# Upsampled attention and token/channel mixer on one core: a table of importance and transfer costs for the list scheduler of the first batch

## The chip, the cores and the metric

The kernel runs on one core of a Trainium2 chip. The metric is device time in microseconds (us) of that core for one execution; lower is better. TensorE is called PE below (PEld where it loads weights), VectorE DVE, ScalarE ACT, GpSimd POOL, and SyncE SP. SP only issues transfers here, and ACT issues four more for each batch.

## The reference

Per batch (8 of them, sequence 576, 8 heads of 64): attention over queries, keys and values averaged in groups of four, repeated back to full length, plus attention in a band of seven positions, and then a mixer over tokens and channels.

```python
out_d = sm_attn(q_d, k_d, v_d)                 # means of 4: 144 x 144 per head
out_up = np.repeat(out_d, factor, axis=2)
mask = np.abs(pos[:, None] - pos[None, :]) < factor
...
x = out_up + out_local                         # (576, 512) per batch
h = np.maximum(xt @ w_tok1, 0.0) @ w_tok2      # token mixing, 576 -> 256 -> 576
u = x + h.transpose(0, 2, 1)
h2 = np.maximum(u @ w_ch1, 0.0) @ w_ch2        # channel mixing, 512 -> 1536 -> 512
return (u + h2).astype(np.float32)
```

## The kernel before

**Work of a batch.** `pooled` (pr 0 to 3) is the averaged attention of two heads each: scores `sd`, `exp` into `pd`, transposes `td`, copy `ptd`, products `ad`, and the result `od`, which four transfers from ACT's queue write into the tiles `vw` of the windowed values. `local` (t 0 to 4) is the band for a tile of 128 rows: scores `sc`, softmax in `P`, transposes `pT`, products `av` with `vw`, and a copy to `x`. `mix` has four generators: `splits` (`x` into high and low parts `xh`), `products` (token products `t1` with W1, then `t2` with W2), `takes` (`hid`, then `u` and its maxima `umx`) and `scaled` (the scaled f16 pair `uh`). The channel products are `c1` (C1 with `uh`, twelve groups f for each half ch of the columns) and `c2` (C2 with `h`). In the trace, `t1` and `t2` both read as `t`, `c1` and `c2` as `c`; buffer numbers are left out.

**Weights.** They arrive as 64-bit words and are turned to f32 once, in the first batch, by `to_f32`: ACT scales the upper words (L210), POOL does two passes (L213, L216), DVE joins them (L221). There are nine pieces of the token weights (W0 to W4 are W1, W5 to W8 are W2; then a cast on ACT, L239, and a difference on DVE, L241), twelve tiles of C1 (raw `C1`, result `CW`) and twelve of C2 (result `CX`, the last `CY`). A tile of C1 or C2 then has its norm summed on PE (`C_sum`), and once a scale is known, `parts` splits it into an f16 pair (L293 on ACT, L295 on DVE). POOL also adds up the averaged values `vr` to `vd` (L409, L410), and for every batch but the first the averaged queries and keys (`pool_q`, L435 to L443). All of this, for the first two batches, shares the five queues with the first batch's attention.

**Order.** Instructions run on each engine in the order in which the program issues them. For the first batch, 75 generators ("streams") are run by a list scheduler, `drive`. A stream yields `step(engine, us, *needs)`: the engine, a cost, what must have been made. `drive` keeps a planned clock for each engine, takes the steps that may go, finds the earliest start, and among those on the same engine within `PATIENCE` of it takes the first of the list; the streams stand in the order of `"LMCTWUDSAmPHaQh"`. Where PE has a planned gap ahead of a product, `keep_busy` fills part of it with products of junk (`busy`). `drive` ends when the first batch's channel mixing and the second's first `uh` are done; from there on, each batch's channel products are run with the next batch's attention in between, a fixed share after each product.

**Streams.** L0 averages the first batch's queries, L1 loads its values, L2, L4 and L5 load the token weights, C1 and C2, L3 its windowed values. C0 to C11, D0 to D11 and W0 to W8 turn tiles of C1, C2 and the token weights; S0 and T0 scale C1 and C2. A0 to A8 are the first batch's attention, M0 to M3 its mix, P0, P1 and Q0 its channel products, U0 to U2 what follows those. H0 loads the second batch, a0 to a8 and m0 to m3 are its attention and mix, h0 loads the third. SP's planned cost is 0.1 us a step, and a load of several transfers is one step.

Of the kernel before, what the change touches and what calls it, by code (L numbers as in the profile page):

```python
# [28 lines left out]
LIVE = 3  # L29
SG = 4  # L30
PATIENCE = 0.15


@with_exitstack
def tile_ups_attention_mixer(ctx, tc, qk, vw, vr, w1, w2, c1, c2, out):

    nc = tc.nc
    B, _, S = out.shape
# [85 lines left out]

    clock = dict(A=2.0, G=5.0, V=2.0, P=0.0, S=0.0, D=0.0)
    now = [0.0]
    free = {k: {i: 0.0 for i in range(n)} for k, n in SLOTS.items()}
    held = {}  # L130
# [21 lines left out]

    def drive(streams, until):

        items = [[g, next(g, None), 0.0] for g in streams]
        driven[0] = True
        while not all(u in made for u in until):
            some = []
            for it in items:
                if it[1] is None or not may(it[1]):  # L160
                    continue
                e, us, needs, at, take, give = it[1]
                if any(not free[k.split('>')[0]] for k in take):
                    continue
                t = max([clock[e], it[2] if at is None else at] + [made[n] for n in needs]
                        + [min(free[k.split('>')[0]].values()) for k in take])
                some.append((t, it))
            best = min(some, key=lambda x: x[0])
            best = next(x for x in some if x[0] <= best[0] + PATIENCE and (x[0] == best[0] or x[1][1][0] == best[1][1][0]))
            t, it = best  # L170
            e, us, _, _, take, give = it[1]
            if e == "P" and ("uh", 0, 1) not in made and free["g"]:
                keep_busy(min(8, int((t - clock["P"]) * 0.6 / 0.22)))
            if e == "P" and ("uh", 0, 0) not in made:
                us *= 1.2
            now[0] = max(now[0], t)
            for x in take:
                k = x.split(">")[0]
                i = now_in[k] = min(free[k], key=free[k].get)
                del free[k][i]  # L180
                held.setdefault((x, None if ">" in x else id(it)), []).append(i)
            clock[e] = t + us
            it[2] = t + us + 0.3
            for x in give:
                i = held[x, None if ">" in x else id(it)].pop(0)
                free[x.split(">")[0]][i] = it[2]
            try:
                it[1] = it[0].send(it[2])
            except StopIteration:
                it[1] = None  # L190
        driven[0] = False
        for k, n in SLOTS.items():
            first = min(free[k], key=free[k].get) if free[k] else [i for (x, _), v in held.items() for i in v if x.split(">")[0] == k][0]
            now_in[k] = (first - 1) % n
        return [it for it in items if it[1] is not None]
# [28 lines left out]
    def weight_loads(pieces, tag, name):  # L224
        raws = {}
        for i, (src, n) in enumerate(pieces):
            yield step("S", 0.1, *([(name, "read", i - BUFS[tag])] if i >= BUFS[tag] else []))
            raws[i] = T([src.shape[0], 2 * n], U32, tag, f"{name}{i}_raw")
            nc.sync.dma_start(raws[i], src)
            made[name, "raw", i] = fetched(src.shape[0] * n * 8)  # L230
            made[name, "raw"] = raws
# [87 lines left out]
    class Second(Channel):  # L319
# [22 lines left out]
        def loads(self):  # L342

            self.raws = made["C2", "raw"] = []
            for i in range(NF):
                if i < 4:
                    yield step("S", 0.1, *(("tile", 0, t) for t in range(len(TILES))))
                    t = T([128, S + KW], F32, "qk", f"C2_raw{i}")[:, :1024].bitcast(U32)
                else:
                    if i % 2 == 0:  # L350
                        yield step("S", 0.1, *(("av", 0, t) for t in range(len(TILES))), *([("C2", "read", i - 4), ("C2", "read", i - 3)] if i >= 8 else []))
                        two = T([128, 2, 1024], U32, "vw", f"C2_raws{i}")
                    t = two[:, i % 2]
                nc.sync.dma_start(t, u32(c2[i]))
                self.raws.append(t)
                made["C2", "raw", i] = fetched(2 ** 19)
# [28 lines left out]
    def load_v(st):  # L385
        st.vd = T([G, 2, H, D + 1], F32, "vd", f"vd{st.b}")
        nc.gpsimd.memset(st.vd[:, :, :, D:D + 1], 4.0)
        ts, arrives = {}, {}

        def fetch(i):  # L390
            pr, g = divmod(i, 2)

            tag = "w" if st.b > 1 else "x" if st.b or i < BUFS["x"] else "xh"
            ts[i] = T([G, 4, 128], F32, tag, f"vr{st.b}_{i}")
            nc.sync.dma_start(ts[i], vr[st.b, g, pr].rearrange("p (r c) -> p r c", r=4))
            arrives[i] = fetched(147e3)

        early = {0: 8, 1: 5}.get(st.b, 0)
        if early:
            yield step("S", 0.1, *([("mixed", 0)] if st.b else []))  # L400
        for i in range(early):
            fetch(i)
        for i in range(8):
            pr, g = divmod(i, 2)
            if i >= early:
                fetch(i)
            t = ts.pop(i)
            e = yield step("G", 1.25, at=arrives[i])
            nc.gpsimd.tensor_add(t[:, 0:2], t[:, 0:2], t[:, 2:4])  # L409
            nc.gpsimd.tensor_add(st.vd[:, g, 2 * pr:2 * pr + 2, :D], t[:, 0].rearrange("p (h d) -> p h d", d=D),  # L410
                                 t[:, 1].rearrange("p (h d) -> p h d", d=D))
            make(("v", st.b, i), e)
# [39 lines left out]
    def pooled(st, pr):  # L452
# [33 lines left out]
        for par in range(2):  # L486
            for g in range(2):
                for kg in range(2):
                    nc.tensor.matmul(ps[:, g, par], pt[:, par, kg, G * g:G * g + G], st.vd[:, kg, 2 * pr + par],  # L489
                                     start=kg == 0, stop=kg == 1)  # L490
        if pr == 0:
            st.od = T([G, 2, 2, 4, D], F32, "od", f"od{b}")
        r = T([G, 2, 2], F32, "sm", f"rd{b}_{pr}")
        e = yield step("V", 0.65, give=one)
# [1 line left out]
        nc.vector.reciprocal(r, r)  # L496
        nc.vector.tensor_tensor(st.od[:, :, :, pr], ps[:, :, :, :D], r.unsqueeze(3).to_broadcast([G, 2, 2, D]),
                                ALU.mult)
        if pr == 3:
            yield step("A", 0.2, ("vw", b), at=e)  # L500
            for h in range(2):
                for par in range(2):
                    nc.scalar.dma_start(st.vw[h][64 * par + 1 + WB:64 * par + KB],
                                      st.od[:, h, par].rearrange("p a d -> p (a d)"))
            make(("full", b), e, 3.0)
        make(("pair", b, pr), e)

    def local(st, t):
# [38 lines left out]
        yield step("A", 0.59, give=one)  # L547
        nc.scalar.copy(pt, ps[:, :4 * n].rearrange("p (hp s) -> p hp s", hp=4))
        make(("tile", b, t), e)
        e = yield step("P", 0.8, ("full", b), ("vw", b), take="gg")  # L550
        ps = P2(f"av{b}_{t}")
        for hp in range(4):
            for j in range(nb):
# [28 lines left out]
    def mix(st):  # L582
# [19 lines left out]
        def products():  # L602
# [8 lines left out]
            for ch in range(2):  # L611
                s0, N = CHUNKS[ch]
                for c in range(4):
                    e = yield step("P", 1.2, ("W", "y", NT + 3), ("hid", b),
                                   *([("over", b - 1, 0)] if b and ch == 0 else []), take="" if c % 2 else f"gg>{b}")
                    if c % 2 == 0:
                        banks[ch, c // 2] = P2(f"t2_{b}_{ch}_{c}")
                    ps = banks[ch, c // 2][:, c % 2, :N]
                    for i, t in enumerate(OF_CHUNK[ch]):
                        o, n = TILES[t][0] - s0, TILES[t][1]  # L620
                        nc.tensor.matmul(ps[:, o:o + n], xf(t)[:, 128 * c:128 * c + 128], ident[:n, :n],  # L621
                                         start=i == 0, stop=False, is_transpose=True, skip_group_check=True)
                    for k in range(2):
                        mm3(ps, lambda a: st.hid[k][:, a, 128 * c:128 * c + 128],
                            lambda a: W2[k][:, a, s0:s0 + N], False, k == 1, skip_group_check=True)
                    make(("t2", b, ch, c), e)
# [71 lines left out]

    def ahead(b):

        yield step("S", 0.1, *([("C2", "read", i) for i in range(4)] + [("pair", 0, 3)] if b == 1 else []))
        st = load(b)
        if b > 1:
            load_w(st)
        yield from pool_all(st)
        yield from load_v(st)
        if b == 1:
            yield step("S", 0.1, *(("C2", "read", i) for i in range(4, NF)))
            load_w(st)

    def side(b):
# [94 lines left out]
        return mixes[b]  # L806

    def windows(st):
        yield step("S", 0.1)
        load_w(st)  # L810

    last = len(TILES) - 1
    with tc.manual_schedule():
# [19 lines left out]
        group["P"] = products[:2]  # L833
        group["Q"] = products[2:]
        group["h"] = [lazily(lambda: ahead(2), ("x", 1, last))]
        streams = [x for k in "LMCTWUDSAmPHaQh" for x in group[k]]
        left = drive(streams, [("over", 0, 1)] + [("uh", 1, 0)] * (B > 1))

    def rest(items):
# [105 lines left out]
```

## Time and profile before

| what | us |
|---|---|
| median of three runs | 963.13 (960.53 to 964.6) |
| span of the profiled execution | 963.2 |
| PE busy in it | 920.6 (96%) |
| DVE, ACT, POOL busy | 440.5, 314.3, 228.5 |

No own time of the profiled execution is listed beside its span; the span agrees with the median within 0.1 us. In the page's second part, each digit is the busy share of a fortieth of the span, some 24 us. A row of the timeline gives start, duration, engine, line, operation, result<-operands, the count, and in brackets the engine's idle time just before and what ended it. A row of a table of windows gives the stretch, its length, then busy time and instructions of each engine, PE's granted clock, the share of the DMA engines and GB/s.

### The profile page before, as it was taken

What the parts mean: (1) busy time and instruction counts of PE and PEld (TensorE: products, weight loads), DVE (VectorE), ACT (ScalarE), POOL (GpSimd) and SP (SyncE); (2) the same over time, 40 slices, a digit from 0 to 9 for tenths busy, and PEclk for the clock granted to TensorE, in tenths of its full rate; (3) what the DMA queues carried; (4) which work ended last, traced back from release to release, by engine and by line L of the source; (5) the groups of instructions that cost most, each with busy time, mean ns of one, the idle gap of its engine ahead of it and who ended that gap; (6) DMA issues with size and microseconds to landing.
All of it is one profiled execution on the core that took longest, in us unless ns stands there. A gap on an engine that the chain in (4) does not pass through costs nothing. (4 is left out here: it accounts for less than half of the span.)

```text
span 963.2 us, 25951 instructions
## 1 busy us (share of the span) xinstructions
PE 920.6 (96%) x11426; PEld 710.8 (74%) x11426; DVE 440.5 (46%) x1058; ACT 314.3 (33%) x723; POOL 228.5 (24%) x361
## 2 busy tenths in 40 slices
PE   6887799999999999999999999999999999999998
PEld 3465577877877788677877778777876778777876
DVE  6777787325352354324453253524453254523221
ACT  2464545214242152314232152413423143422110
POOL 5599960420321003400223003400124000000000
PEclk9777999999999999999999999999999999999999
DMA  8773330620250002500232002500034000000000
GB/s 245 235 278 98 119 80 15 176 64 20 75 155 25 21 20 66 163 14 15 63 126 58 21 9 80 166 7 21 27 82 140 15 14 26 14 1 21 19 12 28
DMA packets 28224, 68.31 MB, mean 71 GB/s; under 512 B 3504, under 2 KB 14000, under 8 KB 26864
## 3 DMA queue, kind: packets, MB, share of 16 engines
q1 hardware_dynamic: 25552, 64.30, 22.0%
q10 hardware_dynamic: 2560, 2.36, 0.9%
q8 instruction: 89, 1.46, 0.6%
q14 instruction: 23, 0.19, 0.1%
HBM read 54.85 MB, written 9.44 MB: 67 GB/s over the span
## 5 line engine op out<-in xcount | busy, mean ns | idle before, releaser
L114 PE MATMUL c<-uh,CW 128*128 128x256 f16 (+1 forms) x2304 | 308.5, 286 | 1.6 <-DVE h L744 1.0
L114 PE MATMUL c<-h,CX 128*128 128x256 f16 (+1 forms) x2304 | 306.9, 286 | 0.0
L114 PEld LDWEIGHTS <-CW 128*128 128x128 f16 x2304 | 216.5, 98 | 68.5 <-issue 15.8
L114 PEld LDWEIGHTS <-CX 128*128 128x128 f16 x2304 | 216.5, 98 | 58.3 <-issue 1.4
L744 DVE SCALAR_TENSOR_TENSOR h<-c,h 128x320 f16<-128x320 f32 (+1 forms) x192 | 87.3, 455 | 161.7 <-ACT h L742 161.6
L742 ACT ACTIVATE h<-c 128x320 f16<-128x320 f32 (+1 forms) x192 | 78.4, 409 | 184.6 <-PE c L114 183.9
L409 POOL TENSOR_TENSOR vr<-vr 72x256 f32<-72x256 f32 x64 | 47.4, 741 | 340.2 <-ACT ptd L483 266.5
L770 DVE SCALAR_TENSOR_TENSOR u<-c,io,u 128x256 f32<-128x256 f32 (+1 forms) x64 | 33.0, 515 | 132.2 <-PE c L114 132.1
L646 ACT COPY u<-t 128x256 f32<-128x256 f32 (+1 forms) x64 | 25.4, 399 | 149.4 <-PE t L114 117.4
L435 POOL TENSOR_TENSOR qs<-qk 128x288 f32<-128x288 f32 x56 | 39.9, 712 | 135.2 <-DMA qk<-in_qk_dram 131.4
L114 PE MATMUL t<-xh,W 128*128 128x512 f32 (+1 forms) x240 | 69.6, 425 | 1.6 <-DVE xh L599 1.4
L648 DVE TENSOR_REDUCE umx<-t 128x1 f32<-128x256 f32 (+1 forms) x64 | 29.2, 457 | 84.8 <-ACT u L646 69.6
L114 PE MATMUL t<-W,hid 128*128 128x256 f32 (+1 forms) x384 | 68.0, 313 | 0.0
L114 PEld LDWEIGHTS t<-W,hid 128*128 128x128 f32 x384 | 54.0, 192 | 2.2
L114 PEld LDWEIGHTS t<-xh,W 128*128 128x128 f32 (+1 forms) x240 | 44.6, 196 | 14.0 <-issue 2.4
L562 ACT COPY x<-av 128x512 f32<-128x512 f32 (+1 forms) x40 | 23.1, 577 | 82.8 <-PE av L557 80.9
L473 ACT ACTIVATE pd<-sd,nmd 72x144 f32<-72x144 f32 x128 | 38.9, 376 | 28.5 <-DVE nmd L468 23.1
L489 PE MATMUL ad<-vd,ptd 72*72 72x65 f32 x512 | 39.4, 229 | 5.1 <-issue 4.7
L489 PEld LDWEIGHTS ad<-vd,ptd 72*72 72x72 f32 x512 | 37.4, 146 | 7.0 <-issue 5.4
L557 PE MATMUL av<-vw,pt 47*32 47x64 f32 x2304 | 35.6, 229 | 5.8 <-DMA vw<-od 3.8
L557 PEld LDWEIGHTS av<-vw,pt 47*32 47x32 f32 x2304 | 27.8, 108 | 16.2 <-issue 8.2
L599 DVE TENSOR_TENSOR xh<-x,xh 128x512 fp32r<-128x512 f32 (+1 forms) x40 | 31.2, 784 | 17.0 <-ACT xh L597 16.9
(107 smaller groups left out, 905.0 us busy)
## 6 DMA issues: line engine op xcount, KB each, us to landing
qk<-in_qk_dram SPq DMA_DIRECT2D x32, 579.0 KB
vw<-in_vw_dram SPq DMA_DIRECT2D x32, 351.0 KB
vr<-in_vr_dram SPq DMA_DIRECT2D x64, 144.0 KB
C_raw<-in_c_dram SPq DMA_DIRECT2D x16, 512.0 KB
out_dram<-u SPq DMA_DIRECT2D x32, 160.0 KB
C_raws<-in_c_dram SPq DMA_DIRECT2D x8, 512.0 KB
out_dram<-u SPq DMA_DIRECT2D x32, 128.0 KB
vw<-od ACTq DMA_DIRECT2D x32, 72.0 KB
```

What stands on the lines that cost most here:

```text
L114: nc.tensor.matmul(ps, lhs(a), rhs(c), start=first and i == 0, stop=last and i == 2, **kw)
L409: nc.gpsimd.tensor_add(t[:, 0:2], t[:, 0:2], t[:, 2:4])
L435: nc.gpsimd.tensor_add(two, x[:, :, 0:2], x[:, :, 2:4])
L473: nc.scalar.activation(pd[:, par, g], s[:, par, g], AF.Exp, bias=nm[:, par, g:g + 1], scale=0.125 / 16)
L489: nc.tensor.matmul(ps[:, g, par], pt[:, par, kg, G * g:G * g + G], st.vd[:, kg, 2 * pr + par], start=kg == 0, stop=kg == 1)
L557: nc.tensor.matmul(ps[QB * j:QB * j + QB, par, D * hp:D * hp + D], pt[p, hp, QB * j:QB * j + QB], st.vw[h][p, g, D * hp:D * hp + D], start ...
L599: nc.vector.tensor_tensor(xh[:, 1], xf(t), xh[:, 0].bitcast(F32), ALU.subtract)
L646: nc.scalar.copy(u, ps)
L648: nc.vector.tensor_reduce(umx[ch][:, c:c + 1], ps, axis=AX.X, op=ALU.max, apply_absolute_value=True)
L742: nc.scalar.activation(ht[:, 0], ps, AF.Relu)
L744: nc.vector.scalar_tensor_tensor(ht[:, 1], ps, 0.0, ht[:, 0], ALU.max, ALU.subtract)
L770: nc.vector.scalar_tensor_tensor(us[c], banks[c], io, us[c], ALU.mult, ALU.add)
```

## The change

It gives each stream a place in a table, `ORDER`. Among the ready steps on the best one's engine within `PATIENCE`, `drive` now takes the one that stands first in the table instead of first in the list, and the rule that a step on any engine goes first if it starts equally early is gone. SP's steps cost `ISSUE` = 0.65 us, and a load of several transfers is a step for each (`C2.loads`, and `load_v` of the first two batches). SP's planned clock starts at 3.0. ACT's step that issues the four transfers of `od` is planned with 2.9 us instead of 0.2 for the first two batches, with the arrival 2.0 us later. Three needs are written out, since the order may now differ: `od` of the other heads, all four pieces of W2, and the tile `od` made by whichever head comes first.

```diff
+ORDER = ("C7 C8 P1 D3 D7 T0 A1 D10 a7 U0 L2 M0 L5 W1 A2 A3 m1 U1 C9 a1 C4 D4 L0 D9 W6 W0 M3 D5 M2 A0 L1 a6 D8 "
...
+ISSUE = 0.65
-    clock = dict(A=2.0, G=5.0, V=2.0, P=0.0, S=0.0, D=0.0)
+    clock = dict(A=2.0, G=5.0, V=2.0, P=0.0, S=3.0, D=0.0)
-        items = [[g, next(g, None), 0.0] for g in streams]
+        items = [[g, next(g, None), 0.0, -ORDER.index(name)] for name, g in streams]
-            best = next(x for x in some if x[0] <= best[0] + PATIENCE and (x[0] == best[0] or x[1][1][0] == best[1][1][0]))
+            best = max((x for x in some if x[0] <= best[0] + PATIENCE and x[1][1][0] == best[1][1][0]),
+                       key=lambda x: x[1][3])
     def weight_loads(pieces, tag, name):
-            yield step("S", 0.1, *([(name, "read", i - BUFS[tag])] if i >= BUFS[tag] else []))
+            yield step("S", ISSUE, *([(name, "read", i - BUFS[tag])] if i >= BUFS[tag] else []))
     # C2.loads: 0.1 becomes ISSUE, and each odd tile is a step of its own
+                    if i % 2:
+                        yield step("S", ISSUE)
     # load_v
-        if early:
-            yield step("S", 0.1, *([("mixed", 0)] if st.b else []))
         for i in range(early):
+            yield step("S", ISSUE, *([("mixed", 0)] if st.b and i == 0 else []))
             fetch(i)
     # pooled
-        if pr == 0:
+        if not hasattr(st, "od"):
             st.od = T([G, 2, 2, 4, D], F32, "od", f"od{b}")
+        make(("od", b, pr), e)
         if pr == 3:
-            yield step("A", 0.2, ("vw", b), at=e)
+            e = yield step("A", 2.9 if b < 2 else 0.2, ("vw", b), *(("od", b, i) for i in range(3)), at=e)
-            make(("full", b), e, 3.0)
+            make(("full", b), e, 2.0 if b < 2 else 3.0)
     # local
-        e = yield step("P", 0.8, ("full", b), ("vw", b), take="gg")
+        e = yield step("P", 0.8 if b else 1.1, ("full", b), ("vw", b), take="gg")
     # products
-                    e = yield step("P", 1.2, ("W", "y", NT + 3), ("hid", b),
+                    e = yield step("P", 1.2, *(("W", "y", NT + i) for i in range(4)), ("hid", b),
     # ahead(1) and windows: 4 * ISSUE for four transfers
-        streams = [x for k in "LMCTWUDSAmPHaQh" for x in group[k]]
+        streams = [(f"{k}{i}", x) for k in "LMCTWUDSAmPHaQh" for i, x in enumerate(group[k])]
```

Three places show how it moves instructions. The rows are those of one engine in the order of the program, before first; in the changed kernel line numbers are 6 to 9 higher (L210 is L217, L213 is L220, L216 is L223).

ACT, at the first tiles of the weights (names with `raw` and L210 or L217 are ACT's scaling; `pt0_0` is the copy of the first band tile's transposes, which PE makes):

```order
L535 ACTIVATE P0_108<-P0_108 128x8x38
L210 ACTIVATE W0_raw_199<-W0_raw_199 128x256
L548 COPY pt0_0_443<-pT0_0_438 128x512
L535 ACTIVATE P1_109<-P1_109 128x8x38
L473 ACTIVATE pd0_2_495<-sd0_2_431,nmd0_2_437 72x144 x4
L548 COPY pt0_1_515<-pT0_1_510 128x512
L483 COPY ptd0_2_527<-td0_2_516 72x576
L239 CAST W1_0_148<-W0_raw_199 128x256
L535 ACTIVATE P2_110<-P2_110 128x8x38
L210 ACTIVATE C10_raw_207<-C10_raw_207 128x512
```

```order
L217 ACTIVATE W1_raw_187<-W1_raw_187 128x256
L217 ACTIVATE W2_raw_195<-W2_raw_195 128x256
L544 ACTIVATE P0_108<-P0_108 128x8x38
L217 ACTIVATE W3_raw_215<-W3_raw_215 128x256
L246 CAST W1_0_148<-W0_raw_183 128x256
L217 ACTIVATE W4_raw_222<-W4_raw_222 64x256
L246 CAST W1_1_149<-W1_raw_187 128x256
L217 ACTIVATE C10_raw_243<-C10_raw_243 128x512
L557 COPY pt0_0_494<-pT0_0_489 128x512
L544 ACTIVATE P1_109<-P1_109 128x8x38
```

Before, the scaling of C1's first tile `C10` stands eight rows behind that of W0 and behind `pt0_0`, `pt0_1` and `ptd0_2`, three copies of what PE has made; now it stands ahead of `pt0_0`, and behind the scalings of all five pieces of W1.

POOL, at the last piece of the token weights, W8 (`C111` is the last tile of C1, `C2_raw0` the first of C2; L213 and L220 are the first pass, L216 and L223 the second):

```order
L213 TENSOR_SCALAR C111_raw_880<-C111_raw_880 128x512
L213 TENSOR_SCALAR W7_raw_807<-W7_raw_807 128x288
L216 TENSOR_SCALAR C111_raw_880<-C111_raw_880 128x512
L216 TENSOR_SCALAR W7_raw_807<-W7_raw_807 128x288
L213 TENSOR_SCALAR W8_raw_874<-W8_raw_874 128x288
L213 TENSOR_SCALAR C2_raw0_1007<-C2_raw0_1007 128x512
L216 TENSOR_SCALAR W8_raw_874<-W8_raw_874 128x288
```

```order
L220 TENSOR_SCALAR C110_raw_849<-C110_raw_849 128x512
L220 TENSOR_SCALAR W8_raw_863<-W8_raw_863 128x288
L223 TENSOR_SCALAR C110_raw_849<-C110_raw_849 128x512
L223 TENSOR_SCALAR W8_raw_863<-W8_raw_863 128x288
L220 TENSOR_SCALAR C111_raw_923<-C111_raw_923 128x512
L220 TENSOR_SCALAR C2_raw0_1006<-C2_raw0_1006 128x512
```

W8's second pass stands ahead of both passes of `C111` and of the first pass of `C2_raw0`, which stood ahead of it.

POOL, at the averages of the second batch's queries and keys (`qs1`, `qd1`), between the tiles 4 to 11 of C2:

```order
L213 TENSOR_SCALAR C2_raws6_1058<-C2_raws6_1058 128x512
L435 TENSOR_TENSOR qs1_0_0_1325<-qk1_0_1248 128x288
L441 TENSOR_TENSOR qd1_1324<-qs1_0_0_1325 128x72 x2
L435 TENSOR_TENSOR qs1_0_1_1329<-qk1_0_1248 128x288
L443 TENSOR_TENSOR qd1_1324<-qs1_0_1_1329 128x144
L216 TENSOR_SCALAR C2_raws6_1058<-C2_raws6_1058 128x512
L435 TENSOR_TENSOR qs1_1_0_1370<-qk1_1_1250 128x288
```

```order
L220 TENSOR_SCALAR C2_raws10_1319<-C2_raws10_1319 128x512
L223 TENSOR_SCALAR C2_raws10_1319<-C2_raws10_1319 128x512
L220 TENSOR_SCALAR C2_raws10_1319<-C2_raws10_1319 128x512
L443 TENSOR_TENSOR qs1_0_0_1457<-qk1_0_1349 128x288
L449 TENSOR_TENSOR qd1_1456<-qs1_0_0_1457 128x72 x2
L443 TENSOR_TENSOR qs1_0_1_1461<-qk1_0_1349 128x288
L451 TENSOR_TENSOR qd1_1456<-qs1_0_1_1461 128x144
L223 TENSOR_SCALAR C2_raws10_1319<-C2_raws10_1319 128x512
L443 TENSOR_TENSOR qs1_1_0_1531<-qk1_1_1351 128x288
```

Before, three of the four averages stand among or ahead of the tiles 7 to 11 of C2; now the first stands inside the last tile, and the others behind it. On SP's queue, the loads of `qk1` move likewise from ahead of C2's tiles 8 to 11 to behind them; on PE, `sd1_0`, `td1_0` and `sd1_1` stand ahead of the first `c1` product before; now `sd1_0` stands behind the fifth group of `c1` (f = 4, ch = 0), `sd1_1` behind the seventh, and `td1_0` still later. Of the norm sums of C2, seven stand behind the first `c1` group instead of four. PE's junk products go from 86 to 79.

More of the change, by code (lines that the diff above doesn't have):

```diff
@@ L31 @@
 PATIENCE = 0.15
+ORDER = ("C7 C8 P1 D3 D7 T0 A1 D10 a7 U0 L2 M0 L5 W1 A2 A3 m1 U1 C9 a1 C4 D4 L0 D9 W6 W0 M3 D5 M2 A0 L1 a6 D8 "
+         "A4 a8 a2 C3 m3 C1 S0 h0 C6 a0 D1 C2 C10 A7 C0 W7 C5 W2 D11 A8 L4 P0 m2 W3 m0 a3 Q0 W8 L3 A5 a5 H0 A6 "
+         "C11 U2 D0 D6 M1 W4 a4 W5 D2 ").split()
+ISSUE = 0.65
 @with_exitstack
@@ L346, in loads @@
                 if i < 4:
-                    yield step("S", 0.1, *(("tile", 0, t) for t in range(len(TILES))))
+                    yield step("S", ISSUE, *(("tile", 0, t) for t in range(len(TILES))))
                     t = T([128, S + KW], F32, "qk", f"C2_raw{i}")[:, :1024].bitcast(U32)
                 else:
-                    if i % 2 == 0:
-                        yield step("S", 0.1, *(("av", 0, t) for t in range(len(TILES))), *([("C2", "read", i - 4), ("C2", "read", i - 3)] if i >= 8 else []))
+                    if i % 2:
+                        yield step("S", ISSUE)
+                    else:
+                        yield step("S", ISSUE, *(("av", 0, t) for t in range(len(TILES))), *([("C2", "read", i - 4), ("C2", "read", i - 3)] if i >= 8 else []))
                         two = T([128, 2, 1024], U32, "vw", f"C2_raws{i}")
@@ L699, in ahead @@
     def ahead(b):
-        yield step("S", 0.1, *([("C2", "read", i) for i in range(4)] + [("pair", 0, 3)] if b == 1 else []))
+        yield step("S", 4 * ISSUE if b == 1 else 0.1, *([("C2", "read", i) for i in range(4)] + [("pair", 0, 3)] if b == 1 else []))
         st = load(b)
@@ L707, in ahead @@
         if b == 1:
-            yield step("S", 0.1, *(("C2", "read", i) for i in range(4, NF)))
+            yield step("S", 4 * ISSUE, *(("C2", "read", i) for i in range(4, NF)))
             load_w(st)
@@ L808, in windows @@
     def windows(st):
-        yield step("S", 0.1)
+        yield step("S", 4 * ISSUE)
         load_w(st)
```

## The prediction

> **What bounds the kernel now.** I read the page's span and engine totals first, then busy times by stretch, then the timeline of the stretch that is not full.
>
> ```profile
> span 963.2 us, 25951 instructions
> PE 920.6 (96%) x11426; PEld 710.8 (74%) x11426; DVE 440.5 (46%) x1058; ACT 314.3 (33%) x723; POOL 228.5 (24%) x361
> ```
>
> PE is busy for 96%, but a slice of that may be junk, so I cut the span at 111.3, where the first `c1` starts; the last row counts junk alone (columns: PE, PEld, DVE, clock, DMA share, GB/s).
>
> ```profile
> core 0: us, PE busy (x) PEld busy (x) DVE busy (x) ACT busy (x) POOL busy (x), PEclk, DMA share, GB/s
> 0.00:111.30 111.30, 85.54 (x1022) 53.90 (x1023) 79.75 (x165) 50.35 (x108) 86.35 (x107) 0.82 0.64 204
> 111.30:140.00 28.70, 27.48 (x300) 22.58 (x301) 24.46 (x55) 15.87 (x36) 25.08 (x33) 1.00 0.38 93
> 140.00:963.20 823.20, 807.60 (x10129) 634.36 (x10116) 336.25 (x839) 248.07 (x581) 117.11 (x222) 1.00 0.18 52
> ...
> 0.00:111.30 111.30, 31.90 (x86) 9.58 (x86) 0.48 (x1) 0.82 0.64 204
> ```
>
> Behind 111.3 PE is full (835.1 of 851.9 us): there only PE work counts, and the order of the later batches stays nearly what it was. Ahead of it PE does 85.54 − 31.90 = 53.6 us of real work in 111.3: this prelude waits for others. So the question is when the first `c1` can start, and what real PE work then lies behind it.
>
> ```profile
> 22.34:48.82 26.48, 20.54 (x344) 12.77 (x348) 18.88 (x41) 11.30 (x28) 13.70 (x15) 0.70 0.76 233
> 48.82:81.30 32.48, 27.43 (x338) 17.23 (x321) 26.02 (x40) 20.31 (x40) 30.49 (x26) 0.72 0.56 200
> ...
> 81.30:111.38 30.08, 21.52 (x141) 15.28 (x142) 20.07 (x45) 13.13 (x28) 28.10 (x28) 0.89 0.45 148
> ```
>
> POOL (the last busy column) works 30.49 of 32.48 and 28.10 of 30.08 us from 48.82 on: it paces the weights. Between 22.34 and 48.82 it works only 13.70. Its waits there, and what stood behind them:
>
> ```profile
> 26.49 0.65 POOL L213 TENSOR_SCALAR C_raw<-C_raw 128x512 uint32<-128x512 uint32 x1 [4.15 <-DMA C_raw<-in_c_dram]
> ...
> 32.85 1.34 POOL L216 TENSOR_SCALAR C_raw<-C_raw 128x512 bf16<-128x512 f32 x1 [5.20 <-ACT C_raw L210]
> ...
> 48.82 1.36 POOL L216 TENSOR_SCALAR C_raw<-C_raw 128x512 bf16<-128x512 f32 x1 [2.40 <-ACT C_raw L210]
> ...
> 23.55 0.86 PE L489 MATMUL ad<-vd,ptd 72*72 72x65 f32 x5 [4.69 <-issue]
> ...
> 26.67 0.58 ACT L548 COPY pt<-pT 128x512 f32<-128x512 f32 x1 [8.80 <-PE pT L544]
> ...
> 42.51 5.08 ACTq L503 DMA_DIRECT2D vw<-od  x4
> ```
>
> 4.15 + 5.20 + 2.40 = 11.75 us. The 5.20 is a chain of order: ACT stood 8.80 us in front of `pt0_0` for PE, which had itself stood 4.69 us, and `C10`'s scaling was queued behind. The 2.40 follows the 5.08 us in which ACT issued the four `od` transfers.
>
> **The end of the prelude.** W8 lets `t2` start, then come `umx`, the scale and `uh`, and `c1`.
>
> ```profile
> 74.41 0.70 POOL L213 TENSOR_SCALAR C_raw<-C_raw 128x512 uint32<-128x512 uint32 x1
> ...
> 76.04 1.34 POOL L216 TENSOR_SCALAR C_raw<-C_raw 128x512 bf16<-128x512 f32 x1
> ...
> 79.67 0.72 POOL L213 TENSOR_SCALAR C_raw<-C_raw 128x512 uint32<-128x512 uint32 x1
> 80.47 0.83 POOL L216 TENSOR_SCALAR W_raw<-W_raw 128x288 bf16<-128x288 f32 x1
> ...
> 104.30 1.33 POOL L216 TENSOR_SCALAR C_raws<-C_raws 128x512 bf16<-128x512 f32 x1
> ...
> 106.70 0.68 DVE L221 SCALAR_TENSOR_TENSOR CX<-C_raws 128x512 uint32<-128x512 uint32 x1
> ...
> 109.37 0.48 DVE L667 SCALAR_TENSOR_TENSOR uh<-u,us,uh 128x256 f16<-128x256 f32 x1
> ...
> 111.38 1.47 PE L114 MATMUL c<-uh,CW 128*128 128x256 f16 x12
> ```
>
> W8's second pass ends at 80.47 + 0.83 = 81.30. DVE joins C2's tiles in order between the steps of `uh`, so POOL paces `uh` too: the tile whose second pass ends at 105.63 is joined at 106.70, the last `uh` at 109.37, and `c1` starts at 111.38, 5.75 us behind that pass.
>
> ```profile
> 83.06:99.50 16.44, 13.93 (x91) 11.36 (x91) 9.00 (x22) 5.49 (x12) 15.49 (x12) 0.90 0.50 148
> ```
>
> Six tiles of C2 (12 passes) take 16.44 us on POOL, 2.74 each.
>
> **The change, part by part.**
>
> *The scaling of `C10` ahead of `pt0_0`.* The 5.20 us wait goes: −5.20. ACT then is late at `pt0_0`, but real PE work has 57.7 us of room there. The other two I leave: raw tiles still come through SP's queue (4.15), and the scaling still shares ACT with the `od` issue (2.40); W pieces now come ahead of some `vr`, which can bring a wait of that size. Bounds: all 11.75 gone, or none, as much coming back as goes.
>
> *W8 ahead of `C111` and `C2_raw0`.* 0.70 + 1.34 + 0.72 = 2.76 us of POOL passes move behind W8. It ends at 81.30 − 5.20 − 2.76 = 73.3.
>
> *Up to `c1`.* `uh` now stands on DVE behind nine tiles: `C111` and eight of C2. 73.3 + 9 × 2.74 = 98.0. The averages of `qs1`, POOL's work ahead of 104.30, are behind them now. For the tail I take 4.0: the 5.75 above without the join of one tile between (0.68) and the 1.07 us the join waited. `c1` starts at 102.0, 9.4 us earlier. Ends: 5.75 again, or 2.0 (from 109.37 to 111.38) where `uh` is ready in time; ±2.
>
> *What moves behind the first `c1`.*
>
> ```profile
> 104.27 0.76 PE L461 MATMUL sd<-qd 64*72 64x144 f32 x8 [2.15 <-POOL qd L443]
> 108.29 0.40 PE L325 MATMUL C_sum<-CX 128*128 128x128 bf16 x4
> 108.52 0.66 PE L480 MATMUL td<-ident,pd 72*72 72x72 f32 x8
> 110.18 0.71 PE L461 MATMUL sd<-qd 64*72 64x144 f32 x8 [1.00 <-POOL qd L443]
> ...
> 115.93 0.38 PE L579 MATMUL C_n_b<-C_n_m,ones 1*128 1x1 f32 x2
> ```
>
> Two `sd`, one `td` and three norm sums go behind the start, one small broadcast goes ahead: 0.76 + 0.71 + 0.66 + 3 × 0.40 − 0.38 = +2.95. These now fill PE where before they lay in its idle time. Seven junk products fewer cost or save nothing: they fill waiting.
>
> *SP's loads as single steps, its cost and its clock; the need on `od`, on W2's four pieces, `hasattr`, the 1.1 for `av`.* They change the plan and so the order only; the transfers are the same in number and size. Nothing by themselves, covered by the order counted above. `qk1`'s loads move behind C2's last two on SP: that is a rival below.
>
> *C2's second half.*
>
> ```profile
> 122.42 0.72 POOL L435 TENSOR_TENSOR qs<-qk 128x288 f32<-128x288 f32 x1
> ...
> 125.07 0.75 POOL L443 TENSOR_TENSOR qd<-qs 128x144 f32<-128x144 f32 x1
> ...
> 160.24 0.74 DVE L295 SCALAR_TENSOR_TENSOR CX<-CY,C_s,CX 128x512 f16<-128x512 f32 x1
> ...
> 161.31 2.79 PE L114 MATMUL c<-h,CX 128*128 128x256 f16 x24
> ```
>
> Before, POOL leaves C2 at 122.42 and its last f16 part ends at 160.98, 38.6 us later, 0.3 ahead of the first `c2`: no slack. After: 98.0 + 4 × 2.74 + 3.4 for one pair of averages between (122.42 to 125.82) = 112.4, parts at 151.0. PE gets to `c2` at about 102.0 + 49.9 + 2.95 less some 4.0 of attention that moves behind (`pT`, `td`, `ad`, two `sc`; estimated from their kind) = 150.8. Even again, so I add nothing; each us of lateness there would cost one.
>
> *Sum.* 963.2 − 9.4 + 2.95 = 956.7, taken as 957 against the profiled span. The median of the runs, 963.13, is 0.1 from it. Bounds: with all waits of POOL gone another −6.55, 950.1; with none gone +5.20, 961.9.
>
> **A rule weighed.**
>
> ```profile
> L213 POOL TENSOR_SCALAR C_raw<-C_raw x16: 642/1128/2353, 26.5 to 88.5; 128x512 uint32<-128x512 uint32 x16
> ...
> L216 POOL TENSOR_SCALAR C_raw<-C_raw x16: 1331/1429/1857, 32.9 to 90.5; 128x512 bf16<-128x512 f32 x16
> ```
>
> The same pass takes 642 to 2353 ns (minimum, median, maximum), so something else stretches it, and with 0.16 us of gaps a tile ((16.44 − 15.49) / 6) it costs between 0.642 + 1.331 + 0.16 = 2.13 and, with the first pass at its median and the second at its longest, 1.128 + 1.857 + 0.16 = 3.15 us. The Trainium skill, "SBUF — State Buffer", the section "SBUF: two separate sides", says that a DVE operation with two inputs in SBUF and a GpSimd operation lock each other out for a whole instruction. By that rule more DVE joins and `uh` beside POOL's passes stretch them, and the sum would be rival C; the spread of the rows agrees with such a lock but does not show which operation holds it.
>
> **The rivals.**
>
> *A. POOL never waits.* For it: ACT's, SP's and the DMA's steps all stand earlier for POOL, and POOL's busy time is unchanged. Against it: the stretch to 48.82 already moves 233 GB/s at a DMA share of 0.76, so data can be late. 950.
>
> *B. The waits come back elsewhere.* W pieces ahead of `vr` delay the averages, ACT's `od` issue still stands in front of a scaling; PE's order is then late at another place. No wait gone: 962, no change that can be measured.
>
> *C. Denser passes stretch each other.* A tile at 3.15 instead of 2.74: nine cost +3.7, 960.4 (at 2.13 they would give 5.5). Also no change to be measured.
>
> *D. Slower: `qk1` is late.* PE takes its work in order, and `sd1_1` now stands behind the seventh group of `c1`; if its averages are late, all of `c1` waits.
>
> ```profile
> DMA packets 28224, 68.31 MB, mean 71 GB/s; under 512 B 3504, under 2 KB 14000, under 8 KB 26864
> ...
> 83.74 9.19 SPq L380 DMA_DIRECT2D qk<-in_qk_dram  x4
> ```
>
> Before, SP issues `qk1` from 83.74 on; after, behind C2's last pair, which waits for the join of two earlier tiles, about 96 by my pace. Two loads of 512 KB and two of 579 KB, 2.2 MB, take 14.7 us at the 148 GB/s of the row from 83.06, 110.7; with POOL free of C2 at 112.4 and one pair more of 3.4, `sd1_1` is ready at 116. PE reaches it at 102.0 + 7 × 1.47 + 5 × 0.40 + 0.76 + small ones, 115.7. Even. At the mean 71 GB/s the data come at 127 and the wait is some 15: 957 + 15 = 972. It decides from a wait of 11 us on (968). Against it: no stretch up to 111 moves that little.
>
> **How the numbers follow.** Within 0.5%, 4.8 us, a measurement of this kernel can hardly tell a change from none: faster is below 958.3, slower above 968. Chances: the sum, 954 to 960, 0.42; A 0.20; B 0.18; C 0.08; D 0.12. Faster: A's 0.20 and three quarters of the sum's case, 0.51. Slower: D, 0.12. The rest, 0.37, is the same. The range of 8 in 10 takes A with a tail 2 us shorter and 1 us of quicker tiles (947), and B with the longer tail's +1.75 and 2 us of lateness at `c2` (966); it leaves out most of D. The likeliest case alone: 954 to 960.
>
> **What would show it.** In the profile of the changed kernel: no wait of POOL for the scaling of `C10`; W8's second pass ending near 73 (78 where B holds, 67 where A); the first `c1` near 102; PE's idle time ahead of `sd1_1` (D) and ahead of the first `c2`, near 151; POOL's time per tile of C2 (C). Real work of PE behind the first `c1` longer by 3 us. I am wrong if PE's row behind the start shows new idle time of more than 2 us, or if the tail from the eighth tile of C2 to `c1` is not 4 us because `um` or another step of the mix sets it.

## The result and the profile after

Four runs of each: 953.49 us (951.28 to 954.76) after, 963.87 us (960.53 to 964.95) before; a ratio of 0.988, interval 0.986 to 0.991, so 8.5 to 14.0 us faster, at the middle some 11. The forecast said 957 (947 to 966). The page of the changed kernel:

```profile
span 949.5 us, 25935 instructions
PE 912.1 (96%) x11419; PEld 707.0 (74%) x11419; DVE 442.4 (47%) x1058; ACT 313.6 (33%) x723; POOL 226.3 (24%) x361
```

Its windows, cut at the first `c1`, with junk alone in the last row:

```profile
0.00:96.98 96.98, 72.68 (x981) 47.78 (x982) 79.64 (x160) 48.82 (x104) 81.69 (x98) 0.89 0.67 210
96.98:949.50 852.52, 839.41 (x10441) 659.20 (x10438) 362.81 (x899) 264.81 (x620) 144.56 (x263) 1.00 0.19 56
...
0.00:96.98 96.98, 24.12 (x79) 7.83 (x79) 0.48 (x1) 0.89 0.67 210
```

The row behind the first `c1` of the kernel before, for the same cut:

```profile
111.38:963.20 851.82, 835.00 (x10405) 656.87 (x10403) 360.63 (x894) 263.94 (x615) 142.11 (x255) 1.00 0.18 54
```

The first `c1` starts 111.38 − 96.98 = 14.40 us earlier. Behind it PE is busy 839.41 − 835.00 = 4.41 longer and idle 16.82 − 13.11 = 3.71 less. −14.40 + 4.41 − 3.71 = −13.70, the difference of the spans. That is 3.3 more than the medians': by its span, the execution profiled of the kernel before is the slowest of its four (964.95, 1.75 above the span), that of the changed one is the fastest of its four (951.28, 1.78 above).

POOL's waits and W8 in the changed kernel (timeline), and the last steps to `c1`:

```profile
15.97 0.77 POOL L223 TENSOR_SCALAR W_raw<-W_raw 128x256 bf16<-128x256 f32 x1 [0.79 <-ACT W_raw L217]
...
42.48 1.34 POOL L223 TENSOR_SCALAR C_raw<-C_raw 128x512 bf16<-128x512 f32 x1 [1.14 <-ACT C_raw L217]
...
68.81 1.34 POOL L223 TENSOR_SCALAR W_raw<-W_raw 128x288 bf16<-128x288 f32 x1
...
91.05 1.39 POOL L223 TENSOR_SCALAR C_raw<-C_raw 128x512 bf16<-128x512 f32 x1
...
96.27 0.68 DVE L676 SCALAR_TENSOR_TENSOR uh<-u,us,uh 128x256 f16<-128x256 f32 x1
...
96.98 2.76 PE L120 MATMUL c<-uh,CW 128*128 128x256 f16 x12
```

Once POOL has begun with the values, its waits sum to 1.93 us where they were 11.75. W8's second pass ends at 70.15 (81.30 before). POOL's whole share shows in one row of windows for each kernel, from its first addition of `vr` to the end of the last second pass that DVE joins ahead of the last `uh` (105.63 before, 92.44 now). Before:

```profile
10.60:105.63 95.03, 71.96 (x960) 48.11 (x957) 68.63 (x134) 46.54 (x99) 77.95 (x79) 0.80 0.64 197
```

The same row of the changed kernel:

```profile
10.71:92.44 81.73, 62.12 (x924) 42.87 (x922) 67.66 (x129) 46.04 (x100) 74.30 (x74) 0.87 0.64 197
```

Of the 13.30 us by which this stretch shrank, 3.65 are busy time (3.25 of them one pair of averages, which is behind now) and 9.65 are gaps (17.08 to 7.43). From there to `c1` it was 5.75 us and is 4.54.

POOL is nearly full from W8 to `c1` in both kernels, so its busy time does not say whether anybody waits for it. The table of DVE's waits does (us in total, times, longest). Before, from 81.30 to 111.38, DVE stood at five joins of C2 for POOL:

```profile
DVE CX L221 <- POOL C_raw L216: 3.8, 2, 2.0
DVE CX L221 <- POOL C_raws L216: 2.7, 3, 1.0
```

In the changed kernel, from 70.15 to 96.98, DVE waits for POOL once, at W8's own join, and is busy for 24.38 of 26.83 us (the third busy time of the row below; 20.07 of 30.08 before). Its waits, and the row of the stretch:

```profile
DVE umx L657 <- ACT u L655: 1.2, 1, 1.2
DVE W_raw L228 <- POOL W_raw L223: 0.7, 1, 0.7
DVE C_inv L291 <- PE C_n_b L588: 0.6, 1, 0.6
DVE umx L657 <- PE t L120: 0.4, 1, 0.4
...
70.15:96.98 26.83, 19.10 (x116) 13.24 (x116) 24.38 (x43) 13.75 (x27) 25.04 (x23) 0.88 0.23 79
```

So up to W8 the gain is in POOL's waits; behind W8 DVE no longer waits for any of POOL's passes, and its own steps fill the way to `c1`.

### The profile page after: what moved, and what is told of

The parts are those of the page before. It is cut to its first block, busy times and chain, and to the rows that moved or that the text cites. A ratio compares the mean times of both kernels' runs of the same rounds, so it can differ in the third digit from the quotient of the medians.

```text
span 949.5 us, 25935 instructions
## 1 busy us (share of the span) xinstructions
PE 912.1 (96%) x11419; PEld 707.0 (74%) x11419; DVE 442.4 (47%) x1058; ACT 313.6 (33%) x723; POOL 226.3 (24%) x361
## 5 line engine op out<-in xcount | busy, mean ns | idle before, releaser
L674 ACT ACTIVATE uh<-u,us 128x256 f16<-128x256 f32 (+1 forms) x64 | 29.8, 524 | 28.1 <-DVE us L126 22.0
```

Of the source, the lines that this page charges most:

```text
L674: nc.scalar.activation(t[:, 0], st.u[ch][c], AF.Copy, scale=s)
```

## The experiments

Two theories were tried first. P: POOL's work and waits ahead of the tile that the last `uh` stands behind set the start of `c1`, microsecond for microsecond. T: the table alone makes the gain. Times are medians, ratios are against the kernel before, run on the same chip.

**The two halves of the change.** The table undone, the new costs kept:

```diff
-        items = [[g, next(g, None), 0.0, -ORDER.index(name)] for name, g in streams]
+        items = [[g, next(g, None), 0.0, -i] for i, (name, g) in enumerate(streams)]
```

> The changed kernel with its table undone: among the ready steps on the best one's engine the first of the old list goes first; all new costs, single loads and clocks stay. Theory P (POOL's work and waits ahead of the tile that the last uh stands behind set the start of c1, microsecond for microsecond): the costs alone put W pieces before the values and know the od issue, so most of POOL's 11.75 us of waits go too, but the second batch's averages stay ahead of the tile in question (some 4.8 us with the first pass beside them) and W8 stands behind more. First c1 near 102, time 957 to 959. Rival T (the table makes the gain, the costs none): as the kernel before, c1 near 111, 963.

965.21 us, ratio 1.002 (1.000 to 1.003): the costs without the table bring nothing, near T's 963; P's 957 to 959 is missed. Timeline:

```profile
30.02 0.72 POOL L417 TENSOR_TENSOR vr<-vr 72x256 f32<-72x256 f32 x1 [3.23 <-DMA vr<-in_vr_dram]
...
80.60 1.34 POOL L223 TENSOR_SCALAR C_raw<-C_raw 128x512 bf16<-128x512 f32 x1 [7.22 <-ACT C_raw L217]
...
109.62 2.50 PE L120 MATMUL c<-uh,CW 128*128 128x256 f16 x12
```

The waits came back elsewhere, and with two smaller ones (0.28, 1.08) they sum to 11.81, as before. The 7.22 is of the old kind: ACT stood in front of copies from PE with the scaling of a tile of C1 queued behind. W8 was early all the same (its second pass ended at 72.60) and did not help.

The table kept, the costs of SP and of the `od` issue as before:

```diff
-ISSUE = 0.65
+ISSUE = 0.1
-    clock = dict(A=2.0, G=5.0, V=2.0, P=0.0, S=3.0, D=0.0)
+    clock = dict(A=2.0, G=5.0, V=2.0, P=0.0, S=0.0, D=0.0)
-            e = yield step("A", 2.9 if b < 2 else 0.2, ("vw", b), ...
+            e = yield step("A", 0.2, ("vw", b), ...
     # and the arrival 3.0 later, the cost of av 0.8, as in the kernel before
```

> The changed kernel with the table and its rule, but SP's steps at 0.1 us, its clock at 0, the od issue at 0.2 and its arrival as before. Theory P: POOL's order then mixes C1 with W from the start and puts averages ahead of most of C2's second half, so POOL waits for data and for ACT again and C2 is late: first c1 106 to 110 and some waiting at the first c2, 960 to 965. Rival T (the table makes the gain): 953 to 955 as the changed kernel.

971.35 us, ratio 1.007 (1.005 to 1.009): slower than either forecast. The first `c1` was at 106.89, earlier than before, but behind it PE was idle for 26.50 us (16.82 before). The longest piece is at the second batch's `av`, where PE stood until `od` had come, as the table of PE's waits says:

```profile
PE av L566 <- DMA vw<-od: 8.0, 1, 8.0
```

So neither half is worth anything alone. T falls with this run, and P has given the time of neither half.

**One cost.** Only the `od` issue at 0.2 again, arrival as before:

```diff
-            e = yield step("A", 2.9 if b < 2 else 0.2, ("vw", b), ...
+            e = yield step("A", 0.2, ("vw", b), ...
-            make(("full", b), e, 2.0 if b < 2 else 3.0)
+            make(("full", b), e, 3.0)
```

> The changed kernel with the od issue planned at 0.2 us on ACT again, and its arrival 3.0 later; all else as changed. W8's second pass moves behind two tiles of C1 that it stood ahead of, and scalings stand behind the od issue without the plan knowing. Theory P: POOL waits 2 to 4 us for the scaling behind the od issue, first c1 99 to 101, 955 to 958. Rival (the od cost decides nothing, as ACT is not full): 953 to 954.

962.64 us, ratio 0.998 (0.997 to 1.000): 9 us lost, more than either theory allowed. A profile of the same kernel:

> Only a profile of the kernel with the od issue planned at 0.2 us, which took 962.6 us: the first one was of an execution with PE slowed down from start to end. Theory P: the first c1 stands some 9 us later than in the changed kernel, near 106, and POOL's waits ahead of it sum to some 9 us more. Rival: c1 near 97 and PE idle behind it.

962.44 us. Timeline:

```profile
43.72 1.33 POOL L223 TENSOR_SCALAR C_raw<-C_raw 128x512 bf16<-128x512 f32 x1 [2.44 <-ACT C_raw L217]
...
80.43 1.16 POOL L223 TENSOR_SCALAR W_raw<-W_raw 128x288 bf16<-128x288 f32 x1
...
111.66 1.47 PE L120 MATMUL c<-uh,CW 128*128 128x256 f16 x12
```

Neither forecast held. The wait behind the `od` issue was 2.44 us, as expected, and all of POOL's waits were only 4.06, 2.1 more than in the changed kernel. But `c1` came at 111.66, 14.7 later: the small change of one cost had moved many other things. W8's second pass ended 11.4 us later, and DVE joined eleven tiles of C2 ahead of `c1` instead of eight. (The span grew by less, 11.1 us, as more of PE's work now lay ahead of `c1`: 835.60 us behind it instead of 839.41.) The price was not the mispriced step's, it was the reordering's. That made a third theory, F: the table is fitted to the exact costs.

**POOL as the pace.** The second pass done twice for six tiles of C2, unknown to the plan, so that no order changes:

```diff
             nc.gpsimd.tensor_scalar(top, hi.bitcast(F32), 2.0 ** -126, 2.0 ** -126, ALU.mult, ALU.mult)
+            if again:      # C2 tiles 0, 1, 3, 4, 5, 6
+                nc.gpsimd.tensor_scalar(top, hi.bitcast(F32), 2.0 ** -126, 2.0 ** -126, ALU.mult, ALU.mult)
```

> The changed kernel with POOL's second pass done twice for six tiles of C2 (0, 1, 3, 4, 5, 6), all ahead of the last uh, unknown to the plan, so that nothing else moves. Six times 1.34 + 0.08 = 8.5 us more on POOL. Theory P: c1 starts 8.5 us later, near 105.5, and the time is 961 to 963. Rival D (the start is set by DVE's and PE's own chain from W8 through umx, the scale and uh, with POOL beside it): c1 up to 3 us later, 953 to 957.

962.85 us, 9.4 more than the changed kernel, and `c1` 9.3 later:

```profile
106.25 2.76 PE L120 MATMUL c<-uh,CW 128*128 128x256 f16 x12
```

The table of DVE's waits from W8's end to `c1` says how the passes got there: DVE, which had waited for POOL at no join of C2, now waited at eight, 12.2 us in all (the two largest entries):

```profile
DVE CX L230 <- POOL C_raw L225: 5.5, 3, 2.3
DVE CX L230 <- POOL C_raws L225: 5.0, 3, 3.0
```

The pass that the eighth join stands behind ended 10.7 us later (103.17 for 92.44) and `c1` only 9.3, so some 1.5 us of POOL's delay cost nothing. P holds for work that is added. Then the first pass of the same six tiles done by ACT, again unknown to the plan:

```diff
-        nc.gpsimd.tensor_scalar(lo, lo, 2.0 ** -29, -0.501, ALU.mult, ALU.add)
+        if by_act:         # C2 tiles 0, 1, 3, 4, 5, 6
+            nc.scalar.activation(lo, lo, AF.Copy, scale=2.0 ** -29, bias=-0.501)
+        else:
+            nc.gpsimd.tensor_scalar(lo, lo, 2.0 ** -29, -0.501, ALU.mult, ALU.add)
```

> The changed kernel with the first pass of the same six tiles of C2 done by ACT instead of POOL, unknown to the plan: POOL gets 6 times 0.65 to 1.1 + 0.08 us less ahead of the last uh, ACT 6 times 0.67 more. Theory P (POOL sets the start of c1): first c1 4 to 6 us earlier, near 92, and the time 948 to 950, less if ACT's steps, which now come between the scalings, become the pace (then 952). Rival D (DVE's and PE's chain from W8 sets it): no earlier start, 953 to 955. C2's integers may differ by how ACT rounds them, which the times do not depend on.

952.74 us, within the spread of the changed kernel. Timeline:

```profile
82.48 2.79 POOL L226 TENSOR_SCALAR C_raws<-C_raws 128x512 bf16<-128x512 f32 x2 [3.22 <-ACT C_raws L221]
...
87.08 1.38 POOL L226 TENSOR_SCALAR C_raws<-C_raws 128x512 bf16<-128x512 f32 x1 [1.04 <-ACT C_raws L217]
...
97.51 0.66 ACT L217 ACTIVATE C_raws<-C_raws 128x512 f32<-128x512 f32 x1 [1.07 <-DMA C_raws<-in_c_dram]
...
99.19 2.76 PE L120 MATMUL c<-uh,CW 128*128 128x256 f16 x12
```

`c1` came 2.2 us later than in the changed kernel, 1.5 of which were there already when W8's second pass ended (71.66). No earlier start is what this rival D has; P's 948 to 950 is missed, and 952, its figure for ACT as the pace, is near. POOL, with less to do, did wait for ACT, and once ACT for a tile of C2 to land. But the trace shows nothing on the way to `c1` that these waits held up: DVE waited for POOL at no join of C2, and was busy for 14.12 of the last 14.19 us:

```profile
85.00:99.19 14.19, 9.89 (x58) 6.84 (x57) 14.12 (x27) 7.79 (x15) 12.04 (x12) 0.85 0.44 157
```

So in the changed kernel POOL is the pace up to W8. Behind W8, POOL and DVE are within some 1.5 us of each other, and DVE is the later one: more work on POOL costs time, less gains none. P holds upward only. No run took work from DVE, so what that would gain is open.

**Places in the table.** The second batch's stream first:

```diff
-ORDER = ("C7 C8 P1 ... A5 a5 H0 A6 "
+ORDER = ("H0 C7 C8 P1 ... A5 a5 A6 "
```

> The changed kernel with one entry of the table moved: H0, the loading and averaging of the second batch, goes to the head. All eight averages then stand on POOL ahead of the second pass of C2's last tile, instead of two; up to the last uh nothing moves. Theory P with its second half (behind the start only PE's order counts): c1 starts at 97 as in the changed kernel, but C2's last norm sum, which stands between the c1 groups, is some 6 to 9 us later and PE waits for it or for c2's weights: 957 to 962. Rival N (the averages' place is worth nothing): 953 to 954.

958.1 us, ratio 0.995 (0.993 to 0.997), within the forecast of P, but not by its reason: behind `c1`, PE waited for none of C2's norm sums, where 6 to 9 us were forecast. Up to `c1` little moved; PE's idle time behind it grew from 13.11 to 18.45 us. The largest single wait is in the second batch's local attention; what the rest has to do with the averages' place is not shown. The row of windows behind `c1`:

```profile
98.21:956.00 857.79, 839.34 (x10442) 660.22 (x10439) 360.25 (x899) 265.61 (x620) 144.48 (x263) 1.00 0.19 56
```

And the timeline of PE:

```profile
154.59 0.63 PE L553 MATMUL pT<-ident,P 128*128 128x128 f32 x4 [2.16 <-DVE P L549]
```

In the kernel before, W's streams ahead of C's:

```diff
-        streams = [x for k in "LMCTWUDSAmPHaQh" for x in group[k]]
+        streams = [x for k in "LMWCTUDSAmPHaQh" for x in group[k]]
```

> The kernel before with one letter of its list moved: the streams of W ahead of those of C (order L M W C T). W8's second pass then stands far ahead of C1's last tiles. Theory P: POOL's work and waits ahead of the tile that the last uh stands behind stay what they were, so that W8's place alone is worth little: c1 109 to 112, 961 to 965. Rival W (W8's place is what the change gained by): c1 10 us earlier, 953 to 956.

960.33 us, ratio 0.996 (0.994 to 0.999). W8's second pass ended at 62.61, 18.7 us earlier than before, and POOL waited as before (5.52 and 5.37 the largest):

```profile
27.10 0.65 POOL L213 TENSOR_SCALAR C_raw<-C_raw 128x512 uint32<-128x512 uint32 x1 [5.52 <-DMA C_raw<-in_c_dram]
...
33.62 1.34 POOL L216 TENSOR_SCALAR C_raw<-C_raw 128x512 bf16<-128x512 f32 x1 [5.37 <-ACT C_raw L210]
...
103.35 1.47 PE L114 MATMUL c<-uh,CW 128*128 128x256 f16 x12
```

`c1` came 8.0 earlier, more than P gave, and 3.1 were lost behind it. POOL accounts for 3.7 of the 8.0 (the pass of the eighth tile of C2 ended at 101.90 instead of 105.63), a shorter way from there to `c1` for the rest, which P does not have. All nine pieces of W moved, not W8 alone; together they are worth some 3 us.

**Theory F against the truth of the costs.**

```diff
-ISSUE = 0.65
+ISSUE = 0.60
```

> The changed kernel with one figure of the plan moved by little: SP's step at 0.60 us instead of 0.65. The plan, with the same table, then puts its first uh 8.4 us later and the end of its list 11.4 us later (its own figures, 100.5 for 92.1 and 220.0 for 208.6). Theory F (the table is fitted to the exact costs, and what the costs say of the chip matters less than that the table was fitted to them): 957 to 963, most of the gain gone. Rival C (the gain is the truer cost of issuing, and 0.60 is as true): 952 to 955.

963.8 us, ratio 0.999 (0.997 to 1.001): the whole gain gone for 0.05 us in one cost of the plan. Timeline:

```profile
48.77 1.33 POOL L223 TENSOR_SCALAR C_raw<-C_raw 128x512 bf16<-128x512 f32 x1 [4.50 <-ACT C_raw L217]
...
97.18 0.65 POOL L220 TENSOR_SCALAR C_raws<-C_raws 128x512 uint32<-128x512 uint32 x1 [3.95 <-DMA C_raws<-in_c_dram]
...
109.34 2.63 PE L120 MATMUL c<-uh,CW 128*128 128x256 f16 x12
```

POOL's waits sum to 11.69 (these, and 0.17, 1.29, 1.27, 0.51), again eleven tiles of C2 are joined ahead of `c1`, and `c1` is 12.4 us late; how that divides between the two is not shown. The rival, that the truer cost made the gain, falls: in the changed kernel's trace the issue of a tile of C1 holds SP's queue for 0.35 us at the median (minimum, median, maximum in ns below), so 0.60 is no further from it than 0.65.

```profile
L236 SPq DMA_DIRECT2D C_raw<-in_c_dram x12: 328/352/812, 11.5 to 49.5; - x12
```

A cost nearer the trace, with a table fitted to it:

```diff
-            e = yield step("A", 2.9 if b < 2 else 0.2, ("vw", b), ...
+            e = yield step("A", 5.0 if b < 2 else 0.2, ("vw", b), ...
     # and another ORDER
```

> The changed kernel with the od issue planned at 5.0 us, near the 5.08 and 6.62 us that the two traces show, instead of 2.9, and the table fitted anew to it by trying some 12,000 changes of places against the plan's own end. The plan's first uh is at 96.9 and its end at 212.0. Theory F: a fitted table gives most of the gain with other costs as well: 952 to 957. Rival C (the truer the cost, the better): under 951. Rival X (only the one table works): 960 or more.

955.19 us, ratio 0.991 (0.988 to 0.994): another table with another cost has most of the gain, as F says; the truer cost adds nothing.

Seven tiles' first pass on ACT, as in the experiment above but known to the plan, and the table fitted to that:

> The changed kernel with the first pass of seven tiles (C1 1 and 5, C2 2, 6, 7, 9 and 10) done by ACT instead of POOL, known to the plan, and the table fitted anew. The plan's end comes 1.5 us earlier (207.0 for 208.6), no more, since its PE has little idle time left behind the first c1. Theory F with theory P: 950 to 953, a us or two under the changed kernel. Rival: the plan's last microseconds do not carry over, 953 to 957.

956.55 us, ratio 0.992 (0.990 to 0.995). The plan's 1.5 us did not carry over. Beside them the changed kernel again:

> The changed kernel once more, beside the other three on the same chip: 952 to 955.

953.32 us, ratio 0.988 (0.986 to 0.991). None was clearly under it. Its profile is a second look at the changed kernel and repeats the first: POOL's waits sum to 2.81 us, DVE is busy for 24.36 of the 26.79 us from W8's join to `c1` without a wait for POOL between, `c1` starts at 97.61, and behind it PE is busy for 839.58 us and idle for 13.21.

## Why the prediction was right

The direction and the place held, and so did the mechanism up to W8: waits of POOL that came from the order went, and `c1` came earlier by them and by what moved behind it. Behind W8 it did not hold: the prediction has POOL pace `uh`, and the trace has DVE. The gain was 10.4 us at the medians for the 6 forecast. By its own steps, with the profile's numbers:

- *The wait in front of `C10` goes*: it did. The term was too small: 5.20 taken, 9.82 measured (11.75 to 1.93). One step that failed is the assumption that the other two stay. Where POOL had waited 4.15 for C1's first tile, it now had W pieces and additions of `vr` to do, and SP issued that tile's load earlier (at 11.46 instead of 13.60). While ACT issued `od`, POOL had passes in hand: the issue took longer (6.62 us instead of 5.08, and ACT stood 8.43 in all, by the rows below), and yet cost POOL 1.14 instead of 2.40. So for the waits it was nearly rival A.

```profile
35.00 6.62 ACTq L512 DMA_DIRECT2D vw<-od  x4
41.67 0.66 ACT L217 ACTIVATE C_raw<-C_raw 128x512 f32<-128x512 f32 x1 [8.43 <-DMA vw<-od]
```

- *W8 at 73.3*: 70.15, earlier by 3.1 of the 4.6 more that the waits gave.
- *Nine tiles at 2.74*: 22.29 us from 70.15 to 92.44, 2.48 each, 2.4 us less in all. The other step that failed is that these passes set `uh`: DVE waited for none of them, so the term came near by luck. The same nine tiles stand on DVE, which is probably why. Even before, the last of the eight joins of C2 stood behind other steps of DVE, with no wait for POOL. Rival C did not show on POOL: the first pass of a `C_raw` tile has a median of 718 ns where it had 1128. It showed on DVE: the join of a tile of C2 has a median of 1062 ns (`C_raws`) where it had 693, and 693 again where DVE waited for POOL (the passes done twice). The Trainium skill, page "SBUF — State Buffer", section "SBUF: two separate sides", states a lock between DVE and GpSimd by which either of them can be held up. The rows fit it, but no run shows which instruction held which.

```profile
L220 POOL TENSOR_SCALAR C_raw<-C_raw x16: 641/718/1732, 23.6 to 90.3; 128x512 uint32<-128x512 uint32 x16
...
L221 DVE SCALAR_TENSOR_TENSOR CX<-C_raws x7: 676/693/1368, 93.8 to 121.3; 128x512 uint32<-128x512 uint32 x7
...
L228 DVE SCALAR_TENSOR_TENSOR CX<-C_raws x7: 804/1062/1228, 84.2 to 101.5; 128x512 uint32<-128x512 uint32 x7
```

- *A tail of 4.0*: 4.54, all of it busy time of DVE, so steps of DVE set it and not POOL. *`c1` at 102.0*: 96.98, by these terms −3.1 − 2.4 + 0.5.
- *2.95 us of real work move behind*: 4.41. The first group of `c1` takes 2.76 us where it took 1.47, at a granted clock of 0.50 where it was 1.00; 2.95 + 1.29 = 4.24. The likely reason is that PE had little to do ahead of it, 1.49 of 3.40 us (2.35 before); no run changes that alone.

```profile
96.98:99.74 2.76, 2.76 (x17) 2.01 (x15) 2.63 (x8) 0.13 (x1) 2.55 (x3) 0.50 0.97 387
99.74:104.00 4.26, 4.26 (x45) 3.80 (x43) 3.39 (x11) 2.62 (x6) 3.86 (x7) 0.93 0.97 360
```

The Trainium skill, page "TensorE: Matmul & The Clock Gate", "Part 1: The HAM clock gate (the "warmup" mystery)", has PE fall to half speed after an idle window of some 3.4 us. The half agrees with the 0.50 of the row; a single gap of that length is not there, as the longest in the last 5 us is 2.10.

- *PE's idle time behind the start unchanged*: it fell by 3.71, a term that I had not set. Together, −5.0 + 1.5 − 3.7 = −7.2 against the sum's 956.7 give the span of 949.5. The three largest misses (the waits, the tiles, the idle time) all went the same way, which is why the gain was larger than forecast.
- *`c2` even with the end of its parts, at 151*: it started at 145.24, with no wait, and the last part ended at 145.73; even, and more than five us earlier.

```profile
144.99 0.74 DVE L302 SCALAR_TENSOR_TENSOR CX<-CY,C_s,CX 128x512 f16<-128x512 f32 x1
...
145.24 1.47 PE L120 MATMUL c<-h,CX 128*128 128x256 f16 x12
```

- *Rival D*: PE met `sd1_1` without a wait.

```profile
111.02 0.71 PE L469 MATMUL sd<-qd 64*72 64x144 f32 x8
```

- *The median 0.1 from the profiled time*: that set a span beside a time. The execution lasted 1.75 us longer than its span, so the 957 against the span stood for some 958.5.

What the prediction did not ask is where the order came from. It read the order as given, which was enough for the time; it could not have told from the diff that the table loses its gain when one cost changes and it is not fitted anew. Open is which pairs of streams carry the gain: moving one entry cost 4.6 us, but no run took the table apart further.

## What to carry to other kernels

Read a scheduler's change from the order it gives, not from its intent: a truer cost and a table that are each worth nothing alone (965 and 971 us) gave 953 together, and 0.05 us in one cost gave all of it back. Where a table has been fitted to a planner, a later change of a cost may need a new fit, and a fitted plan's last microseconds need not carry over. When the busiest engine of a stage is found, look whether the next engine ever waits for it, then add work to it and take work from it: only the second says how much there is to gain.

## What the runs showed that I had not expected

Four transfers issued by ACT held its queue for 5.08 us in the kernel before and 6.62 in the changed one, against 2.93 in the second batch before (row below). Other traffic does not explain it: in these stretches 240, 164 and 60 GB/s were moved, and with the `od` issue planned at 0.2 us the four held the queue for 5.21 us at 46 GB/s. What does is open.

```profile
160.40 2.93 ACTq L503 DMA_DIRECT2D vw<-od  x4
```

And a start that comes earlier can begin cold: the junk products had ended at 92, PE had little else to do up to 96.98, and the first group of `c1` took 1.3 us longer than before.
